# Attention with a spectral filter on one core: a per-key softmax shift with its weight in V, a shorter prologue, and the last group finished by TensorE

## The chip, the cores and the metric

The kernel runs on one NeuronCore of a Trainium2 chip. The metric is the device time of one execution in microseconds (us), shorter is better. In these traces TensorE's clock is at full or at half speed; the share that the profile reports (1.0 or 0.5, or a mean of them) is called the granted clock. Steps and units are counted from 0. Of each kernel, one execution was profiled and several were timed beside the kernel before on the same chip. A run is called slow here when it is over 1.5% above the fastest run of the same kernel. Ratios are the mean time of one kernel's fast runs over the mean time of the other's fast runs of the same rounds, so they are not quite the ratio of the medians quoted beside them.

## The reference

```python
def reference(A_x, A_wqkv, A_wo, B_x, B_w_r, B_w_i, gate_w):   # x: 1 x 2048 x 448, bf16
    x = A_x
    g = sigmoid((x * gate_w).sum(-1, keepdims=True))
    # a: softmax attention, 16 heads of 28
    qkv = (x @ A_wqkv).reshape(B, S, 3, 16, 28).transpose(2, 0, 3, 1, 4)
    p = softmax(einsum("bhqd,bhkd->bhqk", q, k) * 28 ** -0.5, axis=-1)
    a = einsum("bhqk,bhkd->bhqd", p, v).transpose(0, 2, 1, 3).reshape(B, S, D) @ A_wo
    # b: rfft2 of x, times (B_w_r + i B_w_i), irfft2
    return g * a + (1 - g) * b
```

Instead of the maximum of a row of scores the kernel subtracts a bound made of the squared norms of q and k, so that an exponential need not wait for a row to be complete.

## The kernel before

Four heads are worked at a time (T = 0 to 3), 512 queries at a time (b = 0 to 3): 16 groups of 64 units. A unit is 128 keys by 512 queries of one head. ScalarE takes the exponential of three, then two units, alternately: 410 steps. TensorE makes the scores of the next step, multiplies finished exponentials by V ("PV"), and does all the rest (projections, Fourier matmuls) in pieces of about 512 columns that a planner places between the steps.

The norms of K go through a minimum over all keys, and Q gets its bias from it; so all of x and all four blocks of K come before the first score:

```python
    def k_evac(self, T, b, ps, first):
        # ... kT = ps + kone ; sq = kT * kT (first: ScalarE's Square of ps)
    def k_norm(self, T, b, sq, kmin, pool):
        pn = pool([P, QW], F32, name="pn")
        nc.tensor.matmul(pn[:], lhsT=self.selK[:], rhs=sq[:], start=True, stop=True)
        nc.vector.tensor_reduce(out=kmin[:, b:b + 1], in_=pn[:], axis=AX.X, op=ALU.min)
        if b == self.NQ - 1:
            nc.vector.tensor_reduce(out=self.nhk[T][:], in_=kmin[:], axis=AX.X, op=ALU.min)
    # prologue
        turn(0); turn(1); kproj(0)            # turn: transposes of an x block
        # ... projection of Q's block 0
        turn(2); kproj(1); self.k_norm(0, 0, sqk[0], kmin, self.ps_pv)
        turn(3)
        self.q_norm(sqq, sl[2][:, 2, :])
        kproj(2); self.k_norm(0, 1, sqk[1], kmin, self.ps_pv)
        kproj(3); self.k_norm(0, 2, sqk[2], kmin, self.ps_pv)
        self.k_norm(0, 3, sqk[3], kmin, self.ps_pv)
        self.q_bias(0, 0, sl[2][:, 2, :])
```

In the stream, a norm stands well behind the projection it belongs to: K's a block later, Q's three steps later (a yield of three values closes a piece; its last value is the number of steps to wait).

```python
    def do_q(self, T, b):
        # ... four projection matmuls, each followed by a yield
        sq = self.q_evac(T, b, ps[:], False)
        yield 0.213, 512, 3
        # ... q_norm, q_bias
    def do_k(self, T):
        # ... four projection matmuls of block b
            sq = self.k_evac(T, b, ps[:], False)
            yield 0.213, 512, 0
            if prev is not None:
                self.k_norm(T, b - 1, prev, kmin, self.ps_bg)
                yield 0.213, 512, 0
            prev = sq
```

The main loop, and the fillers: a matmul of zeros is put ahead of a step's scores whenever fewer than HEAT = 340 columns of side work per unit were issued. They are there for TensorE's clock: the profiled run of this kernel has a mean granted clock of 0.983.

```python
            ex = nc.scalar.activation(out=ring[:, rp:rp + ne, :], in_=psS[:, 0:ne, :], func=ACT.Exp, scale=self.LN)
            hot = 0
            st["heat"] -= self.HEAT * ne
            if st["heat"] < 0:
                hot = 1
                st["heat"] = max(st["heat"] + 512, -512)
            nxt = qk(s + 1, hot)       # hot fillers, then the scores of the next step
            flush(s)                   # PV of finished exponentials
            # ...
            cols += background(1200)   # pieces of the side work
```

A finished group divides by its sums through DRAM, the last group too:

```python
        nc.vector.tensor_copy(out=oU[:], in_=psPV[:])
        nc.sync.dma_start(out=rs[:], in_=quad_rows(oU[:], m, 32))
        # later: rc = 1 / rs, written to DRAM, read back spread over the partitions as rb
        nc.vector.tensor_tensor(out=self.oT[T][:, QW * b:QW * (b + 1)], in0=oU[:], in1=rb[:], op=ALU.mult)
        # then four matmuls with Wo, the gate and the output, per 128 tokens
```

## Time and profile before

| | before |
|---|---|
| time, median of 3 runs | 510.79 us (509.19 to 511.25) |
| profiled span | 508.9 us |
| first exponential | 23.8 us |
| exponentials, busy | 464.7 us |
| ScalarE idle between exponentials (gaps over 0.1 us) | 1.0 us |
| last exponential to the end | 19.1 us |

Read the table as a sum: 23.8 + 464.7 + 1.0 + 19.1 = 508.6, which is the span but for rounding and gaps under 0.1 us. Every change of the time must show up in one of these terms. The lines of the profile are in the prediction.

### The profile page before, as it was taken

The page shows a single profiled execution, that of the slowest core. Times are in us where ns is not written, and L with a number is a line of the kernel's source. Part 1 is how long each engine was busy: PE and PEld are TensorE (multiplying, and loading weights), DVE is VectorE, ACT ScalarE, POOL GpSimd, SP SyncE. Part 2 cuts the span into 40 slices and gives each one's busy share as a digit, 9 for nine tenths or more (in the row PEclk, how much of TensorE's full clock was granted, in tenths as well). Part 3 has the DMA queues.
Part 4 walks back from the last instruction along what each step waited for, and adds up shares of the span by engine and source line. Part 5 has one row for each costly group of instructions (what it writes and reads, how often), then busy time and mean ns, then how long its engine had stood idle before and what let it go on. Part 6 is the DMA issues. An engine that isn't in the chain of part 4 may idle for free.

```text
span 508.9 us, 7848 instructions
## 1 busy us (share of the span) xinstructions
PE 453.6 (89%) x3306; PEld 159.2 (31%) x3333; DVE 195.5 (38%) x355; ACT 473.3 (93%) x426; POOL 13.8 (3%) x43
## 2 busy tenths in 40 slices
PE   6799999999999999899999999999999999998943
PEld 3433222243233333343333332233233323322211
DVE  3622323422344446645664444423344322322202
ACT  2599999999999999999999999999999999999950
POOL 7100000000000000000000000000000000000000
PEclk9999999999999999999999999999999999999986
DMA  7620000001000012312200000001001011001101
GB/s 244 145 56 9 17 7 4 21 1 30 1 23 0 20 27 51 80 44 66 52 23 13 1 22 23 32 12 34 12 20 34 15 48 32 29 27 32 36 4 55
DMA packets 28138, 17.85 MB, mean 35 GB/s; under 512 B 18568, under 2 KB 25160, under 8 KB 28104
## 3 DMA queue, kind: packets, MB, share of 16 engines
q1 hardware_dynamic: 26184, 17.06, 11.9%
q8 instruction: 26, 0.43, 0.3%
q10 hardware_dynamic: 1920, 0.30, 0.3%
q14 instruction: 8, 0.07, 0.0%
HBM read 15.25 MB, written 1.97 MB: 34 GB/s over the span
## 4 chain that ended last, share of the span: by engine, by line
ACT 85%; PE 8%; DMA 3%; DVE 2%; SPq 1%; issue 0%; ACTq 0%; DVEq 0%
ACT ring L662 85%; PE pf L748 3%; PE psS L549 2%; PE psPV L577 1%; DMA wst_65<-in_A_wqkv_dram 1%; DMA rb<-scr_639 1%; DMA wst_66<-in_A_wqkv_dram 1%; PE psS L564 1%; PE xt L319 1%; DMA rs<-oU 0%; PE pk L256 0%; DVE kT_138 L264 0%; DMA scr_639<-rc 0%; DVE kmin L276 0%; SPq L169 0%
## 5 line engine op out<-in xcount | busy, mean ns | idle before, releaser
L662 ACT ACTIVATE ring<-psS 128x1536 bf16<-128x1536 f32 (+1 forms) x410 | 464.7, 1389 | 4.1 <-PE psS L549 3.6
L577 PE MATMUL psPV<-ring,vsb 128*32 128x512 bf16 x1024 | 102.7, 389 | 0.4 <-ACT ring L662 0.3
L564 PE MATMUL psS<-zero 128*128 128x512 bf16 x219 | 82.6, 377 | 15.0 <-ACT ring L662 12.6
L549 PE MATMUL psS<-qT_136,kT_140 32*128 32x512 bf16 x256 | 40.2, 383 | 6.0 <-ACT ring L662 4.6
L549 PE MATMUL psS<-qT_134,kT_138 32*128 32x512 bf16 x256 | 40.2, 383 | 5.8 <-ACT ring L662 3.9
L577 PEld LDWEIGHTS <-vsb 128*32 128x32 bf16 x1024 | 26.5, 92 | 58.5 <-issue 58.4
L549 PE MATMUL psS<-qT_135,kT_139 32*128 32x512 bf16 x256 | 40.2, 383 | 5.0 <-ACT ring L662 3.7
L549 PE MATMUL psS<-qT_137,kT_141 32*128 32x512 bf16 x256 | 40.1, 383 | 2.0 <-ACT ring L662 1.4
L807 DVE CAST U<-psA 128x512 bf16<-128x512 f32 x32 | 22.0, 691 | 22.9 <-PE psA L803 22.9
L549 PEld LDWEIGHTS <-kT_138 32*128 32x128 bf16 x256 | 12.3, 90 | 44.0 <-issue 41.2
L549 PEld LDWEIGHTS <-kT_141 32*128 32x128 bf16 x256 | 11.4, 90 | 42.7 <-issue 41.6
L549 PEld LDWEIGHTS <-kT_140 32*128 32x128 bf16 x256 | 12.6, 90 | 38.6 <-issue 36.6
L564 PEld LDWEIGHTS <-zero 128*128 128x128 bf16 x219 | 21.4, 98 | 8.5 <-issue 7.5
L549 PEld LDWEIGHTS <-kT_139 32*128 32x128 bf16 x256 | 12.7, 90 | 35.0 <-issue 32.6
L407 DVE CAST vsb<-pvx 128x448 bf16<-128x448 f32 x16 | 10.0, 627 | 32.4 <-PE pvx L403 32.4
L886 DVE TENSOR_SCALAR bm_sb<-psY,omg 128x448 bf16<-128x448 f32 x16 | 10.9, 684 | 29.4 <-PE psY L881 29.4
L719 DVE COPY oU<-psPV 128x512 f32<-128x512 f32 x16 | 11.1, 691 | 26.0 <-PE psPV L577 25.8
L881 PE MATMUL psY<-Binv_sb,ZT 128*128 128x448 bf16 x64 | 20.6, 360 | 0.0
L751 DVE SCALAR_TENSOR_TENSOR fin<-pf,gsb,bm_sb 128x448 bf16<-128x448 f32 x16 | 10.9, 684 | 24.2 <-PE pf L748 24.2
L909 DVE CAST ZT<-psZ 128x512 bf16<-128x512 f32 x16 | 11.1, 691 | 15.9 <-PE psZ L905 15.8
L403 PEld LDWEIGHTS <-xT 128*128 128x128 bf16 x256 | 13.7, 97 | 10.9 <-issue 9.5
L748 PE MATMUL pf<-Wo_sb,qT_137 128*128 128x448 bf16 x16 | 6.5, 408 | 9.1 <-DVE qT_137 L735 9.1
(231 smaller groups left out, 425.2 us busy)
## 6 DMA issues: line engine op xcount, KB each, us to landing
RBg<-cRB SPq DMA_DIRECT2D x16, 128.0 KB, 2.8
rb<-scr_638 SPq DMA_DIRECT2D x8, 256.0 KB
rb<-scr_639 SPq DMA_DIRECT2D x8, 256.0 KB
Wg<-in_B_w_r_dram SPq DMA_DIRECT2D x32, 56.2 KB, 1.9
xtok<-in_A_x_dram SPq DMA_DIRECT2D x4, 448.0 KB, 5.7
out_dram<-fin SPq DMA_DIRECT2D x16, 112.0 KB, 1.7
CSg<-cCS SPq DMA_DIRECT2D x16, 96.0 KB, 1.9
Wg<-in_B_w_i_dram SPq DMA_DIRECT2D x16, 56.2 KB, 2.0
```

Source lines behind the costliest of these rows:

```text
L403: nc.tensor.matmul(pv[:, k, 0:N], lhsT=self.xT[:, c, 128 * t:128 * (t + 1)], rhs=w[:, c, 2 * n0:2 * n0 + N], start=(c == 0), stop=(c == se ...
L549: nc.tensor.matmul(ps, lhsT=self.kT[T][r:r + 32, 128 * i:128 * (i + 1)], rhs=self.qT[T][r:r + 32, QW * b:QW * (b + 1)], start=True, stop=T ...
L564: nc.tensor.matmul(psS[:, 0, :], lhsT=self.zero[:, 0:P], rhs=self.zero[:], start=True, stop=True)
L577: nc.tensor.matmul(psPV[g][r:r + 32, :], lhsT=self.vsb[:, i, 4 * T + j, :], rhs=ring[:, p, :] if isinstance(p, int) else p, start=(count[g ...
L662: ex = nc.scalar.activation(out=ring[:, rp:rp + ne, :], in_=psS[:, 0:ne, :], func=ACT.Exp, scale=self.LN)
L719: nc.vector.tensor_copy(out=oU[:], in_=psPV[:])
L748: nc.tensor.matmul(pf[:, 0:D], lhsT=self.oT[T][:, 128 * t:128 * (t + 1)], rhs=self.Wo_sb[:, T, :], start=(T == 0), stop=(T == self.NTL - 1))
L751: nc.vector.scalar_tensor_tensor(out=fin[:], in0=pf[:, 0:D], scalar=self.gsb[:, t:t + 1], in1=self.bm_sb[:, t, :], op0=ALU.mult, op1=ALU.add)
L807: nc.vector.tensor_copy(out=self.U[:, :, :, :, t * J:t * J + J].rearrange("p b r g j -> p (b r g) j"), in_=ps[:].rearrange("p b (r j) -> p ...
L881: nc.tensor.matmul(psY[:, 0:D], lhsT=Z[0:fn, fb, ri, :], rhs=self.Binv_sb[0:fn, qi, :], start=(qi == 0), stop=(qi == nq - 1))
L886: nc.vector.tensor_scalar(out=self.bm_sb[:, g, :], in0=psY[:, 0:D], scalar1=self.omg[:, g:g + 1], scalar2=None, op0=ALU.mult)
L909: nc.vector.tensor_copy(out=Zs[g][:].rearrange("p b r m -> p (b r m)"), in_=psZ[:].rearrange("p b n -> p (b n)"))
```

## The change

The intent: start the exponentials earlier and end earlier. The shift by K's norms is made per key and put into the scores; to make up for it, V (and the column of ones that gives the sums) is multiplied by the key's weight, exp of the norm relative to the minimum (`do_w`). So the first exponentials need one block of x, of K and of Q. The weights of K and Q are fetched first. The rest of x, K and the weighting move into the stream's first 20 units, V behind them; the ring of exponentials grows from 15 to 33 units, so that PV may come later. Fillers go into the prologue. The last group makes its sums and reciprocals with fp32 matmuls instead of the trip through DRAM. The diff, cut to its core:

```diff
-    RING = 15
+    RING = 33
     HEAT = 340
+    EARLY = 20
@@ load
-        self.load_weights(0, nc.scalar)
+        self.load_weights(0, nc.sync, (0,))      # K
+        self.load_weights(0, nc.scalar, (1,))    # Q
         for b in range(self.NQ):                 # the blocks of x, now on two queues
+        self.load_weights(0, nc.sync, (2,))      # V: the same tile wst
-        self.spread_weights(0, nc.vector)
+        # spread_weights by gpsimd
@@ prologue
-        turn(0); turn(1); kproj(0); ...; self.q_bias(0, 0, sl[2][:, 2, :])   # as shown above
+        hot(self.WARM); turn(0); hot(4)
+        # project K's block 0 and Q's block 0, square each on ScalarE
+        turn(1)
+        self.k_done(0, 0, pk[:], sqk); hot(2)
+        self.q_done(0, 0, pq[:], sqq); hot(5)
@@ do_q (do_k alike, now one block at a time)
-        sq = self.q_evac(T, b, ps[:], False)
-        yield 0.213, 512, 3
-        pn = self.ps_bg([self.P, self.QW], F32, name="pn")
-        self.q_norm(sq, pn[:])
-        self.q_bias(T, b, pn[:])
+        sq = self.square(ps[:], "dve")
+        yield 0.213, 512, 0, 1       # four values: the piece stays open, the norm follows at once
+        self.q_done(T, b, ps[:], sq) # norm matmul into the same PSUM tile, then evacuation
@@ do_v
-            nc.vector.tensor_copy(out=self.vsb[...], in_=pv[...])
+            nc.vector.tensor_tensor(out=self.vsb[...], in0=pv[...], in1=self.wts[T][...], op=ALU.mult)
@@ attention_side
+        yield from self.do_k(0, 1)
+        yield from self.do_x(2, self.ps_pv)
+        yield from self.do_k(0, 2)
+        yield from self.do_x(3, self.ps_pv)
+        yield from self.do_k(0, 3)
+        yield from self.do_w(0)
+        yield from self.do_v(0)
@@ finish_group
+        if g == self.NU // (4 * self.NT) - 1:
+            return self.last_group(psPV, oU, T, b)   # sums, reciprocals, spreading: fp32 matmuls
```

A disused path, which could have made some exponentials on VectorE (its share was set to 0), was taken out as well. Smaller parts of the change that the cut leaves out: the 448 channels of x are cut into four pieces of 112 rows (before: three of 128 and one of 64, padded to 128); the gate is made with the second head group; the planner may place 2000 columns of side work in a step of the first 40 units (before: 1200) and at most two PV groups in a step; the reciprocals of a group are taken a step later.

## The prediction

> **What bounds the kernel now.** I read the page first, then the chain of work that ended last, then ScalarE's groups and waits, then the timelines of the first 24 us and of the end. ScalarE is the busiest engine, and the page's chain says where:
>
> ```profile
> span 508.9 us, 7848 instructions
> PE 453.6 (89%) x3306; PEld 159.2 (31%) x3333; DVE 195.5 (38%) x355; ACT 473.3 (93%) x426; POOL 13.8 (3%) x43
> ACT  2599999999999999999999999999999999999950
> PEclk9999999999999999999999999999999999999986
> ACT 85%; PE 8%; DMA 3%; DVE 2%; SPq 1%; issue 0%; ACTq 0%; DVEq 0%
> L662 ACT ACTIVATE ring<-psS 128x1536 bf16<-128x1536 f32 (+1 forms) x410 | 464.7, 1389 | 4.1 <-PE psS L549 3.6
> ```
>
> The last line is the whole softmax exponential: 410 instructions, 464.7 us busy, 4.1 us idle before them, of which ScalarE's waits put 2.7 us on the very first. So the kernel has three stretches. Start: until the first exponential, read from the chain in order of time:
>
> ```profile
> 8.42 1.05 SPq L169
> 9.51 3.76 DMA wst_66<-in_A_wqkv_dram
> 13.35 1.65 PE xt L319 x16
> ...
> 22.25 0.17 DVE nhk_142 L278
> ...
> 22.52 0.76 DVE qT_134 L296
> ...
> 23.33 0.42 PE psS L549 x3
> ...
> 23.77 46.65 ACT ring L662 x41
> ```
>
> All of x is transposed, all four K blocks projected and the minimum over all keys taken before Q gets its bias at 22.52; the exponentials start at 23.77. Stream: 23.77 to 489.89, 466.1 us, full. End, from the same chain:
>
> ```profile
> 490.32 0.70 DVE oU L719
> ...
> 491.04 1.86 DMA rs<-oU
> ...
> 494.62 4.61 DMA rb<-scr_639
> ...
> 500.07 5.05 PE pf L748 x13
> ...
> 505.15 0.68 DVE fin L751
> ```
>
> That is 508.9 - 489.9 = 19.0 us, of which 8.3 (491.04 to 499.3) is a round trip through DRAM for the reciprocals and 3.1 (505.83 to 508.9) the landing of the last output. The stream can't shrink: same exponentials, same shapes. The gain can only be in the 23.8 and the 19.0.
>
> [...] VectorE's copy of 64x112 weights took 2.49 us beside GpSimd's memset of Wo (1.63 us), while GpSimd's own copies of that size took 0.28. The change gives these copies to GpSimd. [...] PE idles 7.1 to 10.1 us and the granted clock is 0.50 between 11 and 14. The fillers are there for this. [...] no fp32 matmul is in this trace.
>
> **The change, start.** Removed ahead of the first score: transposes of x blocks 2, 3, K projections 1 to 3, four minimum reductions (0.69 each), the Q bias (0.75), a quarter of V. What remains, step by step. The first x block landed at about 3.8 us in the DMA records; now it comes behind 100 KB of K weights and shares the engines (395 GB/s at best, from 4 to 5 us) with blocks 1 and 2: estimate 5.0. 16 transposes at 1.17: 6.2. Four fillers 0.9: 7.0. By then ScalarE's copy (1024 columns, estimate 1.05 from 0.58 for 512) ends at 7.4. K projection of four at 0.21, the last held by that copy: 8.1; Q: 8.9; two squares at 0.60 on ScalarE: 9.5; block 1's 16 transposes lie in TensorE's order before the K norm: 9.9; norm matmuls and two fillers 1.0: 10.9; VectorE's two evacuations at 0.75 end at 11.8, as five fillers do; scores 0.4: **first exponential 12.3**, range 11.8 to 14. That is 11.5 us earlier.
>
> But the removed work is put off, not saved. It now stands in TensorE's order between the scores of the first 15 exponentials (mean 1.14 us a step, 466.1/410), and only two score tiles exist, so TensorE may lag by little over a step before ScalarE idles. From the code's goals (9780 columns of work by unit 20, V by unit 32, 2.5 units a step) the pieces fall so: step 2: K1's norm, all of x2, first K2 matmul; step 4: end of K2, its norm, all of x3; step 6: end of K3 and its norm; steps 11 to 13: five V pieces (1.2) each. A norm can't start until the last projection is out (0.43), copied (0.69) and squared (0.43) by VectorE, with gaps 1.65 after that projection starts. x's pairs share one PSUM bank, so the second pair waits for K's evacuation (0.75) and a copy (0.69). Step 2 thus keeps TensorE from 2.3 to 6.9 us after the first exponential, where ScalarE wanted the scores at 4.6: 2.2 idle. Step 4: to 12.3 against 9.2: 3.1. Step 6: 0.9. Steps 12 to 14, with V and two PV groups (0.33 each) to catch up: 0.8 to 0.9 each. Together 9 in the walk, which takes every wait at its worst; I take **7.5**. Net of the start: -4.0.
>
> **Stream.** Four exponentials of weights (128x64) at about 0.1 in the queue, as the gate's (0.10 in the chain): +0.5. Norm matmuls now follow their projection at once, where before K's came a block later and Q's three steps later. 30 of these lie in the stream. A step leaves room for about 640 columns, a piece is 512, so about a fifth fall in one step with their projection; such a step lasts 0.35 + 0.2 + 1.65 + 0.4 + 0.35 = 2.95 against 2.27 for two exponentials, 0.7 idle: 6 x 0.7 = 4, less what TensorE's slack takes (219 fillers of 0.2 us are in the stream): **+2.5**. VectorE's work is about even: kmin goes (0.69), a raw copy comes (0.69). PE columns grow 2% (258 a unit against 253): no matter.
>
> **End.** PV 0.4; evacuation in halves on two engines 0.45; an output part ahead of the sums keeps TensorE to 0.8; four fp32 sums (estimate 0.3 each) to 2.1; reciprocal 0.25 and spreading 0.6 to 3.1; four fp32 matmuls of 128 columns (estimate 0.5 each) to 5.3; first output part to 5.7; four mixes at 0.68 and two scalings between at 0.2 to 8.5; landing 3.1: 11.6. Against 19.0: **-7.5**.
>
> **Sum.** -11.5 + 7.5 + 0.5 + 2.5 - 7.5 = -8.5: 510.8 - 8.5 = 502.3.
>
> **Rivals.** (a) The put-off work is hidden: TensorE has slack and ring 33 holds 13 steps of exponentials. Then the start gives its 11.5 nearly whole: 510.8 - 11.5 - 7.5 + 2 = 494. For it: 44 us of fillers show slack, and the constants look tuned. Against: slack is spread over 466 us, this work falls in 16, and its waits are for VectorE, not columns. (b) The early stalls cost the whole 9 or more, x or the weights land at 6 to 7 instead of 5, and norms cost 4 in the stream: only the tail is left, 506 to 508. For it: the DMA share was 1.0 from 3 to 6 us already. (c) fp32 matmuls make the tail as long as the DRAM trip: adds 3. Against: that would need over 1 us each, and a 512-column bf16 one takes 0.21.
>
> **Range and chances.** The steps are uncertain by: first exponential 1, early idle 3, stream 2, tail 1; rivals (a) and (b) set 496 to 508. The 2% line is at 500.6, 1.7 below my number and on the side of (a): 0.39 faster, 0.59 same, 0.02 slower.
>
> **What would show it.** First exponential at 12 to 14. ScalarE idle on scores in the first 25 us of the stream: 7.5 in my view, under 2 in (a), in three or four gaps at the x and K blocks. Idle after that: 3, beside norm matmuls that wait for a square. From last exponential to end: 11 to 12.5, without DRAM. Exponentials' busy time unchanged at 465 (within 1). I am wrong if the early gaps are not there, or if PE falls behind steadily instead.

## The result and the profile after

The changed kernel is **slower**: 536.54 us median of 4 runs (531.57 and 527.85 fast; 541.51 and 586.07 slow) against 511.02 of before (509.19 to 514.35). Ratio of the fast runs 1.0358, 95% interval 1.0248 to 1.0468. That is far out of the predicted range of 496 to 508. From the page of the profile after:

```profile
span 529.8 us, 8471 instructions
PE 473.6 (89%) x3437; PEld 163.8 (31%) x3437; DVE 201.5 (38%) x378; ACT 477.0 (90%) x423; POOL 13.3 (3%) x63
ACT  2646799998999999989998999999999998999992
PEclk9757699999999999999999999999999999999999
ACT 45%; PE 31%; issue 12%; DVE 7%; DMA 4%; POOL 0%; SPq 0%; DVEq 0%; ACTq 0%; POOLq 0%
L628 ACT ACTIVATE ring<-psS 128x1536 bf16<-128x1536 f32 (+1 forms) x410 | 471.4, 1268 | 32.1 <-PE psS L555 29.0
```

ScalarE's row has its first full slice in the sixth place now, where before it was the third (a slice is 13 us); the granted clock is at 0.5 to 0.7 in the second to fifth slice; in the chain that ended last ScalarE's share fell from 85% to 45%. The last line gives the cost: the exponentials wait 32.1 us, where before it was 4.1, and they wait for scores. By terms:

| term, profiled runs | before | after | difference | predicted |
|---|---|---|---|---|
| first exponential | 23.8 | 15.8 | -7.9 | -11.5 |
| ScalarE idle, steps 4 to 26 | 0 | 20.9 | +20.9 | +7.5 |
| ScalarE idle later | 1.0 | 10.1 | +9.1 | +2.5 |
| exponentials, busy | 464.7 | 471.4 | +6.7 | +0.5 |
| last exponential to the end | 19.1 | 10.9 | -8.1 | -7.5 |
| sum | | | **+20.7** (span +20.9) | -8.5 |

**The start.** The timeline of the kernel after, from the spreading of K's weights to the scores of step 4 (columns: start, duration, engine, line and operation, count, and in brackets the engine's idle time before it and what ended that):

```profile
9.52 0.56 POOL L255 COPY wk_82<-wst_65 112x448 bf16<-112x448 bf16 x1 [7.22 <-DMA wst_65<-in_A_wqkv_dram]
10.13 1.04 PE L259 MATMUL pk<-xT,wk_82 112*128 112x512 bf16 x4 [1.89 <-POOL wk_82 L255]
...
18.61 0.69 DVE L269 CAST raw<-pk 128x512 bf16<-128x512 f32 x1 [3.27 <-PE pk L259]
19.34 0.42 DVE L270 TENSOR_TENSOR sq<-raw 128x512 bf16<-128x512 bf16 x1
19.82 0.58 PE L275 MATMUL pk<-sq,selK 128*128 128x512 bf16 x1 [0.92 <-DVE sq L270]
20.19 1.06 PE L290 MATMUL xt<-ident,xtok 128*112 128x128 bf16 x8
21.29 0.69 DVE L359 COPY xT<-xt 112x1024 bf16<-112x1024 bf16 x1
...
23.41 0.61 PE L555 MATMUL psS<-qT_160,kT_164 32*128 32x512 bf16 x3
```

The first line: K's weights had landed at 2.9 us by the records of the transfers, yet GpSimd spread them at 9.52, when V's weights had landed, since all three lie in the tile `wst_65` and the wait is for the tile. The rest is the stall at step 4, just in the order in which the prediction walked it: the projection ends, VectorE copies (0.69) and squares (0.42), the norm matmul, two pairs of transposes with VectorE's copy between them, the first matmul of the next projection (cut here), and only then the scores. ScalarE idled from 20.46 to 24.06, 3.60 us; predicted was 2.2. The norm matmul took 0.58 us here, and the scores 0.61 instead of 0.39: the granted clock is half from 19.9 to 47.2 us, and again from 57.4 to 67.6.

**Later.** The timeline at step 154:

```profile
215.98 0.69 DVE L269 CAST raw<-pk 128x512 bf16<-128x512 f32 x1 [2.60 <-PE pk L259]
216.71 0.43 DVE L270 TENSOR_TENSOR sq<-raw 128x512 bf16<-128x512 bf16 x1
217.19 0.38 PE L275 MATMUL pk<-sq,selK 128*128 128x512 bf16 x1 [1.24 <-DVE sq L270]
217.50 0.39 PE L555 MATMUL psS<-qT_161,kT_165 32*128 32x512 bf16 x3
218.00 1.45 ACT L628 ACTIVATE ring<-psS 128x1536 bf16<-128x1536 f32 x1 [1.19 <-PE psS L555]
```

TensorE waits 1.24 us for the square, the scores stand behind the norm in its order, and ScalarE loses 1.19 us. Steps 76 (a Q), 162 and 212 (K) are alike: 1.19, 1.42, 1.19. At step 346 an output block waits for the reciprocals that come through DRAM: 1.39.

**The end.** The timeline of the last group:

```profile
519.79 1.02 PE L747 MATMUL tail_5404<-sum_105,oU 128*128 128x4 f32 x8
521.71 1.13 PE L753 MATMUL tail_5404<-idf,rcl 128*128 128x128 f32 x8 [0.31 <-DVE rcl L751]
```

The trip through DRAM is gone: from the sums (four matmuls, two records each) to the spread reciprocals (four more) it is 3.1 us. The end takes 10.9 us instead of 19.1.

### The profile page after: what moved, and what is told of

It reads as the page before. It is cut to its first block, busy times and chain, and to the rows that moved or that the text cites.

```text
span 529.8 us, 8471 instructions
## 1 busy us (share of the span) xinstructions
PE 473.6 (89%) x3437; PEld 163.8 (31%) x3437; DVE 201.5 (38%) x378; ACT 477.0 (90%) x423; POOL 13.3 (3%) x63
## 4 chain that ended last, share of the span: by engine, by line
ACT 45%; PE 31%; issue 12%; DVE 7%; DMA 4%; POOL 0%; SPq 0%; DVEq 0%; ACTq 0%; POOLq 0%
ACT ring L628 45%; PE psS L555 9%; PE psPV L583 5%; PE psS L570 4%; DVE raw L269 3%; DMA rb<-scr_678 2%; PE pq L259 2%; PE pk L259 2%; DVE sq L270 2%; PE pf L710 1%; DMA wst_65<-in_A_wqkv_dram 1%; PE pvx L401 1%; PE xt L290 1%; PE pq L282 1%; DMA scr_678<-rc 1%
## 5 line engine op out<-in xcount | busy, mean ns | idle before, releaser
L628 ACT ACTIVATE ring<-psS 128x1536 bf16<-128x1536 f32 (+1 forms) x410 | 471.4, 1268 | 32.1 <-PE psS L555 29.0
L570 PE MATMUL psS<-zero 128*128 128x512 bf16 x224 | 86.3, 385 | 14.1 <-ACT ring L628 11.4
L555 PE MATMUL psS<-qT_160,kT_164 32*128 32x512 bf16 x256 | 43.6, 417 | 1.8 <-ACT ring L628 0.8
L555 PE MATMUL psS<-qT_162,kT_166 32*128 32x512 bf16 x256 | 40.2, 383 | 2.8 <-ACT ring L628 1.5
L555 PE MATMUL psS<-qT_161,kT_165 32*128 32x512 bf16 x256 | 40.2, 383 | 2.0 <-ACT ring L628 1.0
L555 PE MATMUL psS<-qT_163,kT_167 32*128 32x512 bf16 x256 | 40.1, 384 | 1.4 <-ACT ring L628 0.8
L555 PEld LDWEIGHTS <-kT_164 32*128 32x128 bf16 x256 | 11.1, 92 | 49.8 <-issue 48.0
L269 DVE CAST raw<-pq 128x512 bf16<-128x512 f32 x15 | 10.4, 691 | 37.3 <-PE pq L259 37.3
L269 DVE CAST raw<-pk 128x512 bf16<-128x512 f32 x15 | 10.4, 691 | 37.2 <-PE pk L259 37.2
L555 PEld LDWEIGHTS <-kT_167 32*128 32x128 bf16 x256 | 11.1, 91 | 42.8 <-issue 41.5
L555 PEld LDWEIGHTS <-kT_166 32*128 32x128 bf16 x256 | 11.5, 91 | 38.2 <-issue 36.7
L555 PEld LDWEIGHTS <-kT_165 32*128 32x128 bf16 x256 | 11.3, 90 | 38.6 <-issue 36.8
L871 DVE TENSOR_SCALAR bm_sb<-psY,omg 128x448 bf16<-128x448 f32 x16 | 10.9, 683 | 28.7 <-PE psY L866 28.7
L866 PE MATMUL psY<-Binv_sb,ZT 128*128 128x448 bf16 x64 | 19.4, 359 | 0.0
L401 PEld LDWEIGHTS <-xT 112*128 112x128 bf16 x256 | 15.3, 105 | 10.6 <-issue 9.8
L893 DVE CAST ZT<-psZ 128x512 bf16<-128x512 f32 x16 | 11.1, 691 | 17.1 <-PE psZ L889 17.1
L705 DVE SCALAR_TENSOR_TENSOR fin<-pf,gsb,bm_sb 128x448 bf16<-128x448 f32 x12 | 8.2, 684 | 21.2 <-PE pf L710 21.2
L275 PE MATMUL pk<-sq,selK 128*128 128x512 bf16 x16 | 6.7, 416 | 9.8 <-DVE sq L270 9.8
```

The lines of the kernel that those rows point to most:

```text
L269: self.nc.vector.tensor_copy(out=raw[:], in_=ps)
L401: nc.tensor.matmul(pv[:, k, 0:N], lhsT=self.xT[:, c, 128 * t:128 * (t + 1)], rhs=w[:, c, 2 * n0:2 * n0 + N], start=(c == 0), stop=(c == se ...
L555: nc.tensor.matmul(ps, lhsT=self.kT[T][r:r + 32, 128 * i:128 * (i + 1)], rhs=self.qT[T][r:r + 32, QW * b:QW * (b + 1)], start=True, stop=T ...
L570: nc.tensor.matmul(psS[:, 0, :], lhsT=self.zero[:, 0:P], rhs=self.zero[:], start=True, stop=True)
L628: ex = nc.scalar.activation(out=ring[:, p0:p0 + ne, :], in_=psS[:, 0:ne, :], func=ACT.Exp)
L866: nc.tensor.matmul(psY[:, 0:D], lhsT=Z[0:fn, fb, ri, :], rhs=self.Binv_sb[0:fn, qi, :], start=(qi == 0), stop=(qi == nq - 1))
```

## What the clock follows

The four runs of the after kernel differ by 58 us, and the granted clock differs with them. From the mean clock c of a run, the time at half clock is 2(1 - c) of its span: 29 us in the run of 527.85, 39 in 531.57, 66 in 541.51 and 192 in 586.07. Over these, by my estimate, each us at half clock goes with about 0.36 us of time ((586.07 - 531.57) / (192 - 39)); with none, the line would end near 518. The slope rests mostly on the one slow run of 586, and none but the run of 531.57 was profiled. So the clock deserved an account of its own, read from the traces.

In after's trace it is half twice between the first exponential and the last. Six stretches of that trace:

| stretch, us | granted clock | TensorE busy, us | matmuls |
|---|---|---|---|
| 14.9 to 19.9 | 1.00 | 3.50 of 5.00 | 19 |
| 19.9 to 47.2 | 0.50 | 22.45 of 27.30 | 140 |
| 47.2 to 52.4 | 1.00 | 5.20 of 5.20 | 64 |
| 52.4 to 57.4 | 1.00 | 3.76 of 5.00 | 31 |
| 57.4 to 67.6 | 0.50 | 10.20 of 10.20 | 41 |
| 67.6 to 72.6 | 1.00 | 4.69 of 5.00 | 32 |

The median record of a score matmul is 0.384 us long at full clock (984 of them) and 0.602 at half (40). The falls, at 19.86 and 57.40, come just after TensorE has waited for VectorE's square: 0.92 us until 19.82, and 1.24 until 56.62. But such a wait was not always followed by half clock. At steps 76, 154, 162 and 212 of the same trace TensorE waited 1.24 us too, and the clock stayed full. Nor does the busy time tell the cases apart: in the 5.00 us that end with the wait of step 154, TensorE was busy for 3.43, less than before either fall. And at half clock it can be busy throughout, as from 57.4 to 67.6.

The profiled run of the kernel before has full clock from 14.3 to 492.2, with TensorE busy for 438.73 of these 477.90 us; yet two of 30 timed executions of before took 525 us at a granted clock of 0.945, so it too can fall. Neither was profiled, and why is open. What tells a wait that is followed by half clock from one that is not was not shown by any run; the experiments below only say where the clock was half, for how long, and what stood before it.

## The experiments

Fourteen kernels ran. The table gives the median, the ratio of fast runs to before of the same chip, and the terms of the profiled run: first exponential; ScalarE's idle time up to step 45 and after it; time at half clock between first and last exponential; end.

| kernel | median us | ratio (95%) | first | idle early | idle later | half clock | end |
|---|---|---|---|---|---|---|---|
| after | 536.54 | 1.0358 (1.0248-1.0468) | 15.8 | 21.1 | 9.9 | 38 | 10.9 |
| b_tail | 503.00 | 0.9862 (0.9836-0.9888) | 23.4 | 0.0 | 1.4 | 0 | 11.0 |
| b_norm | 523.65 | 1.0198 (1.0085-1.0310) | 22.3 | 0.3 | 13.3 | 20 | 18.7 |
| a_warm | 536.97 | 1.0525 (1.0481-1.0568) | 17.2 | 12.1 | 23.7 | 55 | 10.9 |
| a_wake | 519.34 | 1.0156 (1.0101-1.0211) | 17.9 | 11.1 | 5.7 | 10 | 10.9 |
| a_allx | 535.78 | 1.0352 (1.0297-1.0408) | 25.7 | 5.4 | 24.1 | 58 | 10.9 |
| a_ownv | 527.78, 561.85 | two single runs | 13.7 | 13.6 | 16.0 | 31 | 10.9 |
| b_norm_heat | 533.45 | 1.0434 (1.0367-1.0501) | 21.7 | 4.4 | 17.1 | 10 | 18.9 |
| a_heat | 543.34 | 1.0622 (1.0553-1.0690) | 16.1 | 16.9 | 17.1 | 20 | 10.9 |
| b_noheat | 645.85, 614.69 | two single runs | 21.7 | 12.5 | 92.5 | 547 | 19.6 |
| a_best | 535.45 | 1.0485 (1.0454-1.0517) | 17.4 | 21.2 | 10.1 | 65 | 10.9 |
| a_best2 | 530.89 | 1.0299 (1.0168-1.0429) | 15.6 | 17.1 | 8.3 | 34 | 10.9 |
| a_wake_ownv | 518.66 | 1.0155 (1.0107-1.0203) | 14.3 | 13.9 | 6.4 | 24 | 10.9 |
| a_allx_wake_ownv | 516.23 | 1.0116 (1.0075-1.0157) | 22.2 | 4.5 | 6.0 | 10 | 11.0 |
| b_tail_fetch | 500.72 | 0.9824 (0.9713-0.9935) | 19.8 | 0.0 | 1.4 | 0 | 11.0 |

The profiled run of a_allx was a slow one, and so its terms are larger than those of its fast runs (525.87 and 529.89); those of a_best2 and b_noheat were slow ones too. With a mark of 2%, the record calls after, a_warm, a_allx, b_norm_heat and a_heat slower, b_tail and a_allx_wake_ownv the same, a_ownv and b_noheat have no verdict, and the others are unclear; but no interval in the table includes 1.

**The theory:** three causes. The put-off work at the start, with its waits on VectorE in TensorE's order; norms that follow their projection at once; and a clock that is at half for a time behind some of these waits (27.3 and 10.2 us in after), which stretches what runs meanwhile. **The rivals:** that the stalls alone cost it, the clock being a companion; that the per-key shift with its weight in V costs it; and that the clock falls only behind idle time as long as at the start of before, where PE was busy for 0.03 of the 3.00 us from 7.1 to 10.1.

### The parts alone

**b_tail: before, with the last group by TensorE.**

```diff
+        if g == self.NU // (4 * self.NT) - 1:
+            return self.last_group(psPV, oU, T, b)
 # with lead_last, mix, out_part and sum4 as in the change; the side work is emptied two steps before the end
```

> The kernel before with nothing of the change but the last group by TensorE. If the parts add, the stretch from the last exponential to the end falls from 19.1 us to about 11 as in the changed kernel (10.9), nothing else moves, and the time is 511 - 8 = 503. Rival: the forced finish of the background work two steps before the end makes ScalarE idle and takes 2 or more of the 8 back: 505 or more.

Measured: 503.00 (501.62 to 503.84), 0.9862. The end is 11.0, and no other term moved by more than 0.4. This part of the change works as predicted; its rival (505 or more) did not come.

**b_norm: before, with the norms behind their projection.**

```diff
-            yield 0.213, 512, 0
-            if prev is not None:
-                self.k_norm(T, b - 1, prev, kmin, self.ps_bg)
+            yield 0.213, 512
+            self.k_norm(T, b, sq, kmin, self.ps_bg)
 # and in do_q: yield 0.213, 512, 3  ->  yield 0.213, 512
```

> The kernel before with only the places of its norm matmuls changed: K's norm right behind its own projection instead of a block later, Q's without its three steps of delay, as the change has them. Nothing else of the change. If a norm in the same step as its projection stops TensorE for the length of VectorE's evacuation and square, about a fifth of 27 norms give ScalarE a gap of 1.2 us (6 us in all), and each such gap can start a stretch at half clock: 516 or more, the runs apart by over 1.5%, half-clock stretches in mid-stream. Rival (TensorE's slack takes it, the gaps of the changed kernel have another cause): 511, runs within 0.5%.

Measured: 523.65 of six runs (517.93 to 524.73 fast, two slow), 1.0198, some 10 us over before in the fast runs, as expected. Its clock row, and its timeline at step 48:

```profile
PEclk9999995889999999999999999999999999999986
```

```profile
76.06 0.75 DVE L264 TENSOR_SCALAR kT<-pk,kone 128x512 bf16<-128x512 f32 x1 [2.82 <-PE pk L256]
76.85 0.43 DVE L269 TENSOR_TENSOR sq<-kT 128x512 bf16<-128x512 bf16 x1
77.33 0.58 PE L275 MATMUL pn<-sq,selK 128*128 128x512 bf16 x1 [1.30 <-DVE sq L269]
78.50 1.45 ACT L657 ACTIVATE ring<-psS 128x1536 bf16<-128x1536 f32 x1 [1.28 <-PE psS L544]
```

TensorE waits 1.30 for the square, and the clock is half from 77.1 to 94.1: the norm matmul behind the wait took 0.58 us, where one at full clock takes 0.38 (after, step 154). In that stretch lie six more gaps, 5.2 us together; three other gaps are of 1.1 to 1.2 us, and behind one of them the clock is half again, from 107.8 to 111.2. So a clock that falls in mid-stream needs neither the early start nor the weighting: a norm at the wrong place is enough.

### The change with one cause taken out

**a_warm: fillers where TensorE waits at the start.**

```diff
         sq = self.square(ps[:], "dve")
         yield 0.213, 512, 0, 1
+        if T == 0:
+            self.fill(4)
         self.k_done(T, b, ps[:], sq)
 # and self.fill(5) between the two halves of do_x; fill(n): n matmuls of zeros into a tile of its own
```

> The changed kernel with fillers put where TensorE waits in the first 15 us of the stream (4 ahead of each K norm of the first head group, 5 between the two halves of each lift of x); no wait is removed. Clock theory [...]: the clock stays at 1.0 from 20 to 68 us, the gaps before steps 4, 6 and 8 shrink from 3.6, 4.6, 2.4 to about 2.3, 3.1, 0.9, those from step 13 to 27 (10 us together) mostly vanish, the time is near 518 and the runs agree within 1%. Rival (the waits alone, whatever the clock): gaps and time stay, 528 or more, and the runs spread as before.

Measured: 536.97 (533.83 to 538.96), missed by 19. At the start it did as expected; the timeline shows steps 4 and 6 at full clock:

```profile
24.16 2.36 ACT L637 ACTIVATE ring<-psS 128x1536 bf16<-128x1536 f32 x2 [2.37 <-PE psS L564]
...
29.47 2.37 ACT L637 ACTIVATE ring<-psS 128x1536 bf16<-128x1536 f32 x2 [2.95 <-PE psS L564]
```

The gaps of steps 4, 6 and 8 are 2.37, 2.95 and 1.04; after had 3.60, 4.61 and 2.39; the prediction's walk said 2.2, 3.1 and 0.9. So for these three steps the walk was right at full clock, and the half clock made the rest. Early idle fell from 21.1 to 12.1. But the same norm gaps as in after (steps 76, 154, 212: 1.19 each, 162: 1.42) are still there, and now the clock fell behind three of them: it is half from 120 to 134, 226 to 243 and 291 to 308 us. In after's trace it fell behind none of the four; what makes the difference was not shown.

**a_wake: the norm held back one step.**

```diff
-        yield 0.213, 512, 0, 1
+        yield 0.213, 512, 1, 1
 # and in background: an open piece whose time has not come ends the round
+                if k is not None and wake[k] > st["cur"]:
+                    break
```

> The changed kernel with each norm held back to the step after its last projection (the open piece sleeps one step). If the gaps of 1.2 to 1.4 us in the later stream come from a norm that stands in TensorE's order right behind its projection, those vanish: idle after 80 us falls from 9.4 to about 3. In the start the norms of the second and third K block move out of the crowded steps: idle there falls from 21.6 to some 15. Together 520 or so, still with a half clock in the start. Rival (the later gaps are too many columns for a step): idle after 80 us stays at 9.

Measured: 519.34 (515.87 to 523.92), 1.0156. The gaps of 1.2 to 1.4 us at steps 76, 154, 162 and 212 are all gone; idle later fell from 9.9 to 5.7, early from 21.1 to 11.1, half clock from 38 to 10. In the fast runs this one edit takes back some 10 of the 18 us (1.0358 to 1.0156, on different chips).

**a_allx: all of x and K's four blocks in the prologue again.**

```diff
+        k1 = kproj(1)
+        turn(2)
+        k2 = kproj(2)
+        self.k_done(0, 1, k1[0][:], k1[1])
+        turn(3)
+        k3 = kproj(3)
+        self.k_done(0, 2, k2[0][:], k2[1])
+        hot(4)
+        self.k_done(0, 3, k3[0][:], k3[1])
 # attention_side begins at do_w(0); goals: weights by unit 6, V by 32
```

> The changed kernel with all of x transposed and all four K blocks projected before the first score, as before the change; per-key shift, weight in V, ring of 33 and the new tail stay. If the put-off work causes the early gaps, the first exponential moves from 15.8 to about 22 to 24 us, no gap before the V stretch, idle there under 4 (from 21.6), and the time is near 511 (start even with before, tail -8, later stream +8). Rival (the per-key shift or the ring is at fault): early gaps of 10 us or more remain and the time stays above 520.

Measured: 535.78 (525.87 to 542.17), far over the expected 511; even the fast runs missed by 15 and 19. Early idle fell to 5.4, as the theory has it, and the first exponential came at 25.7. But in the profiled run the norm gap of step 212, again 1.19, was followed by half clock for 48 us. Two stretches of that run, before and behind that gap (columns: stretch, length, busy us of PE, PEld, DVE, ACT and POOL with instructions, granted clock, DMA share, GB/s):

```profile
254.00:280.00 26.00, 23.73 (x198) 9.05 (x198) 13.83 (x31) 25.47 (x23) 0.00 (x0) 1.00 0.21 50
283.00:309.00 26.00, 25.30 (x113) 5.99 (x111) 9.05 (x17) 18.07 (x16) 0.00 (x0) 0.50 0.00 2
```

TensorE is busy for 25.30 of 26 us at half clock and gets 113 matmuls done instead of 198; ScalarE gets through 16 instructions instead of 23. In after's trace the gap of the same step was 1.19 as well, and the clock stayed. If a gap is followed by half clock in some executions and not in others, that would make after's runs scatter; it is not shown for after itself, whose slow runs were not profiled.

**a_ownv: V's weights in a tile of their own.**

```diff
-                          12 * self.Dh + 1], BF16, name=f"wst{i}")
+                          8 * self.Dh], BF16, name=f"wst{i}")
+        self.wv = [per.tile([self.DP, self.NDC, 4 * self.Dh + 1], BF16, name=f"wv{i}") for i in range(2)]
```

> The changed kernel with V's weights of each head group in a tile of their own, nothing else. If GpSimd's spreading of K's weights waits for V's weights only because they share a tile, it moves from 9.5 to about 6 us; the first K projection then waits for ScalarE's copy of x alone (9.2 us), and the first exponential comes at about 14.9 instead of 15.8. Rival (the weights land that late): unchanged 9.5 and 15.8. The time changes little, because the early gaps stay.

Measured: first exponential at 13.7 instead of 15.8; two runs, 527.78 and 561.85. The wait for V's weights was a false one, and cost 2.1 us (expected: 0.9). The time says nothing with two runs so far apart.

### The fillers and the clock

**b_noheat: before without fillers in the stream.**

```diff
-    HEAT = 340
+    HEAT = 0
```

> The kernel before without any filler in the stream, a wrong turn on purpose to see what they do. [...] the clock is half for most of the stream[...]: 560 or more. Rival (clock follows how long TensorE is busy): busy share is 0.75 or so without fillers, the clock stays, and the time is 511 or a little less.

Measured: 645.85 and 614.69. Busy time and the rows of TensorE, ScalarE and the clock, from its page:

```profile
PE 599.6 (93%) x3087; PEld 162.3 (25%) x3114; DVE 195.7 (30%) x355; ACT 504.8 (78%) x426; POOL 13.9 (2%) x43
...
PE   8899999999999999999999999999999999787963
...
ACT  4778878787887888787787887887887887999870
...
PEclk9755555555555555555555555555555555999565
```

TensorE is 93% busy, no less than in any other of these kernels, and is at half clock for 547 us of the stream, 526 of them in one piece. The expectation of 560 or more held, its rival is out. So a busy TensorE did not keep the clock up here. What it is about the fillers that goes with the full clock was not shown; what was measured is a mean granted clock of 0.563 and 0.638 without them, against 0.967 to 0.990 in the seven runs of before on the same chip.

**b_norm_heat and a_heat: more fillers.** The same edit in b_norm and in after:

```diff
-    HEAT = 340
+    HEAT = 420
```

> The kernel with only the norms moved, with about a quarter more fillers (a filler when under 420 instead of 340 columns of work came per score tile). [...] So the gaps of 1.2 us stay, 6 or so, the half-clock stretches go, time 517 to 519 and all runs within 0.7%. Rival (the wait itself drops the clock, whatever the fillers): half-clock stretches and a spread from 518 to 535 as before.

> The changed kernel with the same one number changed (340 to 420). The start is as it was, since there the fillers are held off by the columns of the projections: idle of about 20 us to step 27, partly at half clock. After that no half-clock stretch in any run: the slow executions of 541 and 586 do not come again, the runs lie within 1.5% of each other, 524 to 532. Rival: runs over 540 come again.

Measured: b_norm_heat 533.45 (532.41 to 535.24), a_heat 543.34 (541.73 to 544.54). The half of the expectation on the clock nearly held: no half clock in b_norm_heat's stream but from 23.3 to 33.5, in a_heat's later stream only from 218.3 to 221.7, and the runs of both agree within 0.6%, where b_norm's span 3% and after's 11%. The half on the time failed: both are slower. b_norm_heat has 53 gaps of 21.5 us where b_norm has 27 of 13.6: TensorE is near full, and each further filler stands ahead of some step's scores. So fillers are no cure for a stall; they swap it for smaller ones.

### Versions put together

**a_best: after with V's tile apart, x2 and x3 lifted in the prologue, norms two steps later; a_best2: the same with more fillers.**

```diff
-        yield 0.213, 512, 0, 1
+        yield 0.213, 512, 2, 1
-        hot(2)
+        turn(2)
         self.q_done(0, 0, pq[:], sqq)
-        hot(5)
+        turn(3)
+        hot(2)
 # goals: K by unit 18, weights by 26, V by 45; output blocks two steps later
 # a_best2 also: HEAT 600 in the first 30 units, 420 afterwards
```

> The changed kernel with what the runs so far point to: V's weights in a tile of their own, x blocks 2 and 3 lifted before the first score, norms held back two steps, V spread over 19 units instead of 12, output blocks two steps later. First exponential near 17 (one less from the weights, one to two more from the lifts), idle in the first 30 steps 3 to 5 (from 11.6 with norms held back one step), later idle 2 to 3 (from 5.3), clock at 1.0 from the start of the stream to the end, time 503 to 506. Rival (the early projections and V still do not fit beside the scores): 510 or more.

> The mended kernel of the second series (V's weights apart, x lifted before the first score, norms two steps later, V spread) with more fillers: under 600 columns a tile in the first 30 units, under 420 later. [...] the clock does not fall at 31 us, the V stretch has idle of 3 or less instead of 20 up to step 45, the second stretch at 253 us does not come, time 502 to 506. Rival (the fillers take TensorE's time where it is full already): idle moves to other steps and the time stays over 515.

Measured: 535.45 and 530.89; both missed. The first ten steps run without a gap, but then V and the PV that waited for it come together: 2.72 at step 13 in both, 2.3 to 2.5 at step 25, and the clock is half from 31 to 92 us in a_best but for ten. The work that was moved did not vanish, it met ScalarE a little later.

**a_wake_ownv and a_allx_wake_ownv: two and three causes taken out together** (the edits above).

> The changed kernel with norms held back one step and V's weights apart, the put-off work left in the stream. First exponential at 14 (a_ownv: 13.7), idle in the first 30 steps near 11 as with the norms alone held back (11.4), later idle 5: 14 + 466 + 16 + 5 + 11 = 512. If it comes at or above the run with all three removed, the early start of the exponentials earns nothing on this kernel.

> The changed kernel with the three causes removed at once: x and K ahead of the first score, norms held back one step, V's weights apart. Per-key shift, weight in V, ring of 33 and the new tail stay. If the three are the whole cause: first exponential near 23, idle in the stream 6 to 8 (4 in the V stretch, the rest small), no half clock after the start, end at 23 + 466 + 8 + 3 + 11 = 511 or less, all runs within 1%. Rival (the per-key shift, the weight in V or the ring cost of their own): 516 or more, or half-clock stretches in mid-stream.

Measured: 518.66 (514.86 to 520.74) and 516.23 (514.35 to 518.38), ratios 1.0155 and 1.0116. Both missed, by 7 and by 5. The first starts its exponentials 8 us before the second (14.3 against 22.2) and idles 9.4 us more in its first 45 steps: the early start earns nothing. The second is the change without its three faults, and is still over before, though it has the new end. Its account against before: first exponential -1.6, idle +9.5, exponentials +5.7 (470.4 against 464.7), end -8.0; the sum, +5.6, is the profiled 514.7 against 508.9 but for 0.2. The idle time is 4.5 at the start, where V must wait for the weights and they for all of K, and 6.0 in some 20 small gaps later. Of the 4.5, some 3 lie at half clock (25.6 to 35.8); the largest of the later gaps is the output block of step 346 again (1.11; before 0.18). The rival's mark, 516 or more, was met. So what is left of the change costs something by itself: the per-key shift, the weight in V, the ring, the planner's new limits, or the half clock at the start; no run separates them. By how much: b_tail has the same end, and over it the changed kernel is 25 us longer (1.0358 - 0.9862 of 511), this version 13. The three causes carry about half of that loss, and the other half stays open.

**b_tail_fetch: before with the new end, K's and Q's weights fetched first, V's in a tile of its own, x on two queues.**

```diff
+        self.load_weights(0, nc.sync, (0,))
+        self.load_weights(0, nc.scalar, (1,))
         for b in range(self.NQ):
-            nc.sync.dma_start(...)
+            (nc.sync, nc.scalar)[b % 2].dma_start(...)
+        self.load_weights(0, nc.sync, (2,))       # into self.wv, not wst
 # on top of b_tail
```

> The kernel before with the new tail and with K's and Q's weights fetched first, V's after x in a tile of its own, x from two queues. Weights are spread at 4 to 5 us instead of 7.3, the first K projection runs at about 8 instead of 10.1; the rest of the old start is bound by the last x blocks and the chain of norms. First exponential near 22 (from 23.4), time 501 to 502 against 503 with the tail alone. Rival (the landing of x bounds the old start): no change, 503.

Measured: 500.72 (499.19 to 505.40) against 510.94 on the same chip, ratio 0.9824. The interval is wide (0.9713 to 0.9935), as two runs of before on that chip took 525. From its timeline:

```profile
7.99 1.22 PE L265 MATMUL pk<-xT,wk 128*128 128x512 bf16 x4
...
19.84 1.45 ACT L671 ACTIVATE ring<-psS 128x1536 bf16<-128x1536 f32 x1 [2.71 <-PE psS L558]
```

The first projection starts at 7.99, and the first exponential is 3.9 us earlier than before; the stream has no half clock and 1.4 us of idle time. It has the lowest median of this study and is ahead of both kernels (the record calls it unclear at the 2% mark); over b_tail, which ran in an earlier series on the same chip, it gains 2.3 us at the medians and 3.5 in the profiled runs, and the two intervals overlap.

## Why the prediction was wrong

**What bounds the kernel** was read rightly: ScalarE in the stream, 23.8 before it and 19.0 behind it. **The end** was right in its steps and its sum: -8.1 measured, -7.5 said. The fp32 matmuls were cheaper than the prediction's estimates, which had none in the trace to rest on: 0.25 and 0.28 us each instead of 0.3 and 0.5. b_tail shows this part alone.

**The first exponential** came at 15.8, not at 12.3. The weights: the walk let K's projection follow the lifting of x, at about 7; it began at 10.13, as the spreading waited for V's weights in the same tile. a_ownv puts that at 2.1 us; the rest is x, whose transposes began at 6.28 and not at 5.0.

**The early idle, predicted 7.5, was 20.9.** This is the step that failed, in three ways. The prediction took its own walk of 9 as the worst case and cut it to 7.5; a_warm shows that the walk was close for steps 4 to 8 (6.4 measured, 6.2 said), so nothing was to be cut. The walk had 2.6 for steps 12 to 14 and nothing after; a_warm has 5.6 from step 12 to 20, where V, the PV behind it and Q's norm crowd. Together that is 12 us, of waits mostly at full clock (a_warm's was half from 34.8 to 41.6, over steps 12 and 13). The other 9 us went when fillers kept the clock up: that is the half clock, of which the walk had no notion.

**The norms, predicted +2.5, cost twice that as waits, and can cost more through the clock.** The walk said six cases of 0.7, less TensorE's slack; there were four of 1.2 to 1.4 (5.0 together), so fewer but longer ones, and no slack shortened them. The rest of the later idle time is the output block of step 346 (1.39), which the prediction did not have, and small gaps (3.7). In after's trace the clock did not fall behind these four; in b_norm, a_warm and a_allx such a gap brings 3 to 48 us at half clock.

**The exponentials' busy time, predicted +0.5, rose by 6.7.** "Unchanged within 1" was wrong. The page's sum counts once what two records overlap, and the traces show what that does: an exponential of 1536 columns whose record begins over 0.15 us before the last one ends adds 1.343 us, one without overlap 1.451 (of 1024 columns: 0.917 and 1.024). Without overlap are 15 of the 410 before and 55 after, some 0.107 us each: 4.3 of the 6.7. The rest, 2.5, lies in records that overlap by less. So each exponential that has to wait for its scores costs a tenth of a us on top of its idle time, and the prediction had no term for that.

**The clock.** The prediction had one observation of it, half clock from 11 to 14 us behind a PE that idled from 7.1 to 10.1, and took the fillers as harmless slack ("44 us of fillers show slack"). The second is refuted: b_noheat has a TensorE that is 93% busy, and half the clock for 547 us. And the one observation did not say how short a wait can be: in b_norm the clock fell within a wait of 1.30 us. The change put waits where there had been none, four of 1.24 us in after's later stream among them. Rivals (a) and (b) of the prediction stayed too near to it, since neither had a term that multiplies.

**The theory's own rivals.** That the stalls alone cost it: no, since a_warm takes 4.2 of 10.6 us out of the gaps at steps 4 to 8 with the same waits in them. That the weight in V and the schedule around it cost it: in part, as 13 us over b_tail are left when the three causes are out. But the share of each, stall and clock, in b_norm's 10 us is not settled: b_norm_heat keeps the clock up and loses more time to its fillers.

## What to carry to other kernels

Work that is put off past the start is free only if the engine that feeds the bottleneck can do it without waiting for anyone: count the waits in that engine's order, not the columns, and let two dependent matmuls stand a step apart. Read the granted clock beside TensorE's busy time: here it was half for 547 us of a run in which TensorE was 93% busy (b_noheat), and 17 us at half clock began in one wait of 1.30 us (b_norm). Runs that scatter with the granted clock were the sign of it: after's four lie 11% apart, at clocks from 0.836 to 0.972. And give separately awaited transfers separate tiles, or fetching one first may gain nothing: here the shared tile cost 2.1 us at the start (a_ownv).
